# Two heads side by side on the halves of the rows, for the scores of groups two to four

## The chip, the cores and the metric

The kernel runs on one core of one Trainium2 chip. The metric is device time in microseconds (us) of one execution. A core has TensorE (matmuls, with their weight loads), VectorE (DVE), ScalarE (ACT), GpSimd (POOL) and SyncE (SP), and 16 DMA engines. SP and POOL issue nearly all transfers of this kernel.

## The reference

The output joins two results along the last axis. The first is attention with sixteen query heads on one key head and one value head; the second is a filter in the frequency domain.

```python
B, S, D, H = 1, 2048, 448, 16;  Dh = D // H          # Dh = 28
q = (x @ wq).reshape(B, S, H, Dh).transpose(0, 2, 1, 3)
k, v = x @ wk, x @ wv
p = softmax(einsum("bhqd,bkd->bhqk", q, k) * Dh ** -0.5)
a = einsum("bhqk,bkd->bhqd", p, v).transpose(0, 2, 1, 3).reshape(B, S, H * Dh) @ wo
X = rfft2(B_x) * (w_r + 1j * w_i)
b = irfft2(X, s=(S, D))
return concatenate([a, b], axis=-1)
```

All inputs and outputs are float32.

## The kernel before

**Splitting into high and low parts.** Large products run in the one-pass type float32r, which rounds its operands. To keep float32 accuracy an operand is split into a high part (its rounded value) and a low part (the rest). A head has 28 dimensions, padded to 32, so four strips of 32 rows fill the 128 rows of TensorE. The keys lie in `ka`, 128 x 2048: high, high, low, low. A head's queries lie in `qa[c, g][:, h]`, 128 x 512: high, low, high, low. One matmul of 128 rows (L807) sums all four products of the parts.

**Groups, steps, blocks.** The 2048 queries are cut in four chunks `c` of 512 and the sixteen heads in four sets `g` of four. One pair (c, g) is a group; there are sixteen, in the order of `order`. A group has sixteen steps, one for each 128 keys (`kc`), and a step has four scores, one for each head `h`. So there are 256 steps and 1024 scores.

**A score** (`score`, L803): a matmul of 128 keys by 512 queries into one of the seven banks 0 to 6 of PSUM (the one that the plan holds to be free first), then on ScalarE the exp of that bank into a tile `p` (L809). **Values** (`values`, L821): for each step four float32 matmuls of 32 columns, side by side, add the four heads' products into bank 7 (L828). At a group's end VectorE copies bank 7 out (`group_out`, L704), and the next group's values can't start before that copy. Then come the reciprocal of the sums (through DRAM and back, `sd`, `rs`, `rd`, `R`: L709 to L718, issued from POOL) and the norm (L726 to L729).

**The queries of a group** (`build_q`, L166): VectorE makes the high and low parts `qh` and `ql` (L171 to L173). SP issues eight transfers of 64 KB that place them in rows 0 to 63 of the four heads (L182), and one of 512 KB that copies rows 0 to 63 to rows 64 to 127 (L183). The tiles of two groups take turns.

**The frequency part.** A first transform runs ahead of the attention and leaves its result in DRAM (`t1`). During the attention POOL issues eight loads of `X` from it (`spread`, L487), loads of the filters `wf` (L571) and of `wo` (L475). VectorE splits `wo` (L478, L479), and runs the butterflies on `X` and the filter products (L502 to L585). The last transform and the products with `wo` (L738) are done by TensorE between the scores.

**What sets the order.** From L435 on the order of every engine is written out by a planner at build time. It keeps clocks for TensorE, VectorE and ScalarE (`clk`), the times at which banks come free (`free`), and events with due times (`after`). Its main loop (L881) chooses between scores, values and other TensorE work. It holds the scores at most `P_BUFS` = 20 tiles `p` ahead of the values (L887). A block in the steady part is eight scores and two steps of values. The order is fixed at build time: on the chip every engine works through its list and waits where something is not ready.

Of the kernel before, what the change touches and what calls it, by code (L numbers as in the profile page):

```python
# [12 lines left out]
F32 = mybir.dt.float32  # L13
F32R = mybir.dt.float32r
BF16 = mybir.dt.bfloat16
I32 = mybir.dt.int32
AF = mybir.ActivationFunctionType
# [5 lines left out]
S, D, H = 2048, 448, 16  # L23
# [4 lines left out]
CW = 512  # L28
NK = 4
SCALE = DH ** -0.5  # L30
BOUND = float(np.float32(40.0 / SCALE))
P_BUFS = 20
LEAD = 6
WARM = 10, 10


@with_exitstack
def kernel(ctx: ExitStack, tc: tile.TileContext, t: dict):
    nc = tc.nc
    mm = nc.tensor.matmul  # L40
# [13 lines left out]
    ka = cp.tile([128, S], F32R, name="ka")  # L54
# [7 lines left out]
    bank = [bp.tile([128, 512], F32, name=f"b{i}") for i in range(8)]  # L62
# [7 lines left out]
    def spin(*dims):  # L70
        return view(bank[next(turn) % 6], *dims)
# [83 lines left out]
    qa, slots = {}, []  # L155
# [10 lines left out]
    def build_q(c, g, first=False):  # L166
        cs = slice(c * CW, (c + 1) * CW)
        qt = qp.tile([128, CW], F32, name="qt")
        qh = qp.tile([128, CW], F32R, name="qh")
        ql = qp.tile([128, CW], F32R, name="ql")  # L170
        nc.vector.tensor_scalar(qt, qraw[:, g, cs], mask, cvec[:, g, c:c + 1], op0=ALU.mult, op1=ALU.add)  # L171
        nc.vector.tensor_copy(qh, qt)
        nc.vector.tensor_tensor(ql, qt, qh.bitcast(F32), op=ALU.subtract)  # L173
        n = 4 * c + g
        if len(slots) <= n < 2:
            slots.append((qp if n == 0 else ap).tile([128, 4, CW], F32R, name=f"qa{n}", bufs=1))
        q = qa[c, g] = slots[n % 2]
        if first:
            return q, qh, ql
        for i in range(4):  # L180
            for p, src in enumerate((qh, ql)):
                nc.sync.dma_start(q[32 * p:32 * p + 32, i].bitcast(F32), src[32 * i:32 * i + 32].bitcast(F32))  # L182
        nc.sync.dma_start(q[64:128].bitcast(F32), q[0:64].bitcast(F32))  # L183
# [3 lines left out]
    with tc.tile_pool(name="f1", bufs=2) as f1[0], tc.tile_pool(name="w1", bufs=1) as w1:  # L187
# [36 lines left out]
        with tc.tile_pool(name="x1", bufs=2) as x1:  # L224
# [5 lines left out]
            nc.vector.memset(idle, 0.0)  # L230
            for n in WARM:
                nothing = spin(512)
# [94 lines left out]
            for c in range(1, NC):  # L327
                for g in range(NG):
# [22 lines left out]
                    n = 4 * (c - 1) + g  # L351
                    if n in places:
                        q = places.index(n)
# [40 lines left out]
        with tc.If(rv > int(np.float32(BOUND).view(np.int32))), tc.tile_pool(name="g1", bufs=1) as g1:  # L394
# [10 lines left out]
            with tc.For_i(0, 64, 1) as n:  # L405
# [3 lines left out]
                for i in range(4):  # L409
                    r = slice(32 * i, 32 * i + 32)  # L410
# [4 lines left out]
                pt = banks[1][:, :128]  # L415
# [3 lines left out]
            nc.vector.memset(cvec, 0.0)  # L419
            nc.vector.memset(mask, 1.0)  # L420
            parts = build_q(0, 0, True)
            q, qh, ql = parts
            for i in range(4):
# [13 lines left out]
    ap = ctx.enter_context(tc.tile_pool(name="ap", bufs=2))  # L437
    pp = ctx.enter_context(tc.tile_pool(name="pp", bufs=P_BUFS))
# [3 lines left out]
    clk = {"pe": 0.0, "dve": 4.0, "act": 0.0, "mode": "s", "new": False}  # L442
    free = [0.0] * 6 + [2.0]
# [3 lines left out]
    def after(when, dur, f, *a):  # L447
        heapq.heappush(events, (when, next(serial), dur, f, a))

    def vector(until):  # L450
        while clk["dve"] < until:
            if events and events[0][0] <= clk["dve"]:
                _, _, dur, f, a = heapq.heappop(events)
                clk["dve"] += dur
                f(*a)
            elif background and background[0][0] <= clk["dve"]:
                _, dur, f = background.popleft()
                clk["dve"] += dur
                f()
            else:  # L460
                clk["dve"] = min([until] + [x[0] for x in (*events[:1], *list(background)[:1])])
# [5 lines left out]
    wol = ap.tile([128, NG, D], F32R, name="wol", bufs=1)  # L467
    fc["cs3"] = ap.tile([113, 4, 113], F32, name="cs3", bufs=1)
    nc.gpsimd.dma_start(fc["cs3"], t["cs3"])

    wo = {}

# [226 lines left out]
    oh, ol, osb = {}, {}, {}  # L699
# [64 lines left out]
    def switch(mode):  # L764
        if clk["mode"] != mode:
            clk["pe"] += 0.093
            clk["new"] = True
            clk["mode"] = mode

    def spent(dur):  # L770
        if clk["new"] and clk["mode"] == "s":
            dur += 0.105
        clk["new"] = False
        clk["pe"] += dur

    def can_fill():
        return cur[0] is not None or bool(work["z"]) or bool(work["w"])
# [22 lines left out]
    pt, end = {}, [0.0] * 1024  # L800
    EARLY = 6

    def score(i):  # L803
        st, h = divmod(i, 4)
        c, g, kc = steps[st]
        b = min(range(7), key=free.__getitem__)
        mm(bank[b], ka[:, kc * 128:(kc + 1) * 128], qa[c, g][:, h], start=True, stop=True)  # L807
        p = pt[i] = pp.tile([128, CW], F32, name="p")
        nc.scalar.activation(p, bank[b], AF.Exp, scale=SCALE)  # L809
        clk["pe"] = max(clk["pe"], free[b])  # L810
        switch("s")
        a = max(clk["act"], clk["pe"] + 0.54 + (0.1 if clk["new"] else 0.0))
        spent(0.2325)
        clk["act"] = a + 0.477
        end[i] = a + 0.593 + 0.06
        free[b] = a + 0.593 + 0.05
        n = 4 * c + g
        if kc == 0 and h == 0 and n + 1 < len(order):
            after(clk["pe"] + 3.0, 1.7, build_q, *order[n + 1])

    def values(o, n):  # L821
        while taken_out[0] < o // 16:
            vector(clk["dve"] + 0.5)
        switch("v")
        for st in range(o, o + n):
            c, g, kc = steps[st]
            for i in range(4):
                mm(bank[7][32 * i:32 * i + 32], vs[:, kc], pt.pop(4 * st + i), start=(kc == 0), stop=(kc == 15))  # L828
            clk["pe"] = max(clk["pe"], end[4 * st + 3]) + 0.86
            if kc == 15 and st < 255:  # L830
                after(clk["pe"] + 0.4, 0.72, group_out, c, g)
        clk["new"] = False
# [8 lines left out]
    def first_fill():  # L841
        pb = fft1_mm(7)
        clk["pe"] += 1.6
        free[6] = inf
        fft1_out(7, pb)
        clk["dve"] = max(clk["dve"], clk["pe"] + 0.5) + 1.5
        free[6] = clk["dve"] + 0.1

    for g in range(NG):
        after(5.0 + 6 * g, 0.0, wo_load, g)  # L850
        after(11.0 + 6 * g, 1.1, wo_split, g)
# [3 lines left out]
    sc, bt, begun, since, gap = 0, 0, False, 0, 2  # L855
    parts, tail = deque((k, g) for k in range(4) for g in range(NG - 1)), {}

    def partial():
        k, g = parts.popleft()
        if g == 0:  # L860
            b = min(range(7), key=free.__getitem__)
            clk["pe"] = max(clk["pe"], free[b])
            free[b] = inf
            tail[k] = bank[b][:, :D]
        switch("s")
        wo_mm(tail[k], NC - 1, k, (g,))
        spent(0.605)

    def size():
        left = 16 - done_steps % 16  # L870
        rich = sum(map(len, work["w"])) * 0.6 + len(work["z"]) * 0.88 + (len(cur[0][0]) * 0.6 if cur[0] else 0.0) > 1.0
        return left if left < 4 else 2 if left == 4 or not rich else 3
# [3 lines left out]
    def share(n):  # L876
        return max(1.2, 3 * (total - done[0]) / max(250 - done_steps, 3)) if n == 3 else 0.0

    done_steps, quota = 0, 0.0
    n = size()  # L880
    while done_steps < 256:  # L881
        if begun:
            vector(clk["pe"])
        need = 4 * (done_steps + n)
        t_v = end[need - 1] if sc >= need else inf
        soon = min(free) <= clk["pe"] + 0.05
        more = sc < 1024 and sc - 4 * done_steps < P_BUFS  # L887
        if not begun and not soon:
            first_fill()
            begun = True  # L890
        elif t_v <= clk["pe"] + 0.05 and (sc >= min(need + LEAD, 1024) or not soon):
            values(done_steps, n)
            done_steps += n
            n = size()
            since, gap, quota = 0, 2, share(n)
        elif can_fill() and quota > 0 and since >= EARLY and gap >= 2 and (cur[0] or soon):
            t0 = done[0]
            fill()
            quota -= done[0] - t0
            gap = 0  # L900
        elif more and soon:
            score(sc)
            sc += 1
            since += 1
            gap += 1
        elif sc == 1024 and can_fill():
            fill()
        elif sc == 1024 and parts and normed[NC - 1] == NG - 1 and t_v > clk["pe"] + 0.5:
            partial()
        elif t_v <= min(free) or not more:  # L910
            values(done_steps, n)
            done_steps += n
            n = size()
            since, gap, quota = 0, 2, share(n)
        else:
            score(sc)
            sc += 1
            since += 1
            gap += 1
    while can_fill() or events or background:  # L920
        while can_fill():
            fill()
# [2 lines left out]
    c, g = NC - 1, NG - 1  # L925
# [8 lines left out]
    for k in range(4):  # L934
        s = o[:, 128 * k:128 * k + 128]
        r = ap.tile([128, 128], F32, name="r", bufs=1)
# [122 lines left out]
```

## Time and profile before

| what | us |
|---|---|
| median of 3 runs | 649.89 |
| lowest and highest run | 648.18 and 650.11 |
| the profiled execution | 647.86 |
| its span, first to last instruction | 646.0 |
| around the span | 1.86 |
| TensorE busy | 634.9 |
| ScalarE busy | 548.4 |
| VectorE busy | 331.9 |

A row of the profile gives the line of the kernel, the engine, the operation, the tiles written and read, the count, and times. PEld is TensorE's weight load, which overlaps its matmuls. Matmuls are pipelined: their records overlap, and the distance from one start to the next is what a matmul costs in a row of them. The exps overlap in the same way, so that their recorded length is more than what one costs. A row of the timeline shows the start, the length from the first start to the last end, and in brackets the idle time ahead with what ended it. Float32 matmuls appear as two records each.

### The profile page before, as it was taken

The page shows a single profiled execution, that of the slowest core. Times are in us where ns is not written, and L with a number is a line of the kernel's source. Part 1 is how long each engine was busy: PE and PEld are TensorE (multiplying, and loading weights), DVE is VectorE, ACT ScalarE, POOL GpSimd, SP SyncE. Part 2 cuts the span into 40 slices and gives each one's busy share as a digit, 9 for nine tenths or more (in the row PEclk, how much of TensorE's full clock was granted, in tenths as well). Part 3 has the DMA queues.
Part 4 walks back from the last instruction along what each step waited for, and adds up shares of the span by engine and source line. Part 5 has one row for each costly group of instructions (what it writes and reads, how often), then busy time and mean ns, then how long its engine had stood idle before and what let it go on. Part 6 is the DMA issues. An engine that isn't in the chain of part 4 may idle for free.

```text
span 646.0 us, 11674 instructions
## 1 busy us (share of the span) xinstructions
PE 634.9 (98%) x4384; PEld 356.8 (55%) x4384; DVE 331.9 (51%) x685; ACT 548.4 (85%) x1101; POOL 91.0 (14%) x170
## 2 busy tenths in 40 slices
PE   8999899999999989999999999999999999999997
PEld 6877544444444436555445665565555655555654
DVE  6999612599896797887921512130343403120233
ACT  4544899999999978888999888889888798979792
POOL 2021040201011211010131201010201201010100
PEclk9999999999999989999999999999999999999999
DMA  8756499512204322030685231312334231310111
GB/s 276 260 159 176 119 244 192 137 34 51 68 18 105 123 63 64 23 90 15 151 217 149 91 81 46 82 32 65 98 108 113 82 81 31 81 47 1 47 44 57
DMA packets 31162, 63.35 MB, mean 98 GB/s; under 512 B 7093, under 2 KB 18918, under 8 KB 29884
## 3 DMA queue, kind: packets, MB, share of 16 engines
q1 hardware_dynamic: 23168, 39.98, 22.9%
q0 software_dynamic: 7360, 21.69, 12.5%
q8 instruction: 35, 0.57, 0.4%
q10 hardware_dynamic: 576, 0.92, 0.4%
q14 instruction: 23, 0.19, 0.1%
HBM read 30.56 MB, written 15.02 MB: 71 GB/s over the span
## 4 chain that ended last, share of the span: by engine, by line
PE 81%; issue 2%; DVE 2%; DMA 2%; POOL 0%; ACT 0%; ACTq 0%; SPq 0%; DVEq 0%; POOLq 0%
PE b L807 37%; PE b L828 34%; PE b L738 6%; PE b L679 2%; PE b L660 2%; DMA wf<-w 1%; DVE w L579 1%; DMA t<-bs 1%; ACT yb L743 0%; DMA rd<-rs 0%; POOL R L718 0%; DVE X L585 0%; DVE qraw L704 0%; PE b L136 0%; ACTq L748 0%
## 5 line engine op out<-in xcount | busy, mean ns | idle before, releaser
L809 ACT ACTIVATE p<-b 128x512 f32<-128x512 f32 x1024 | 506.9, 743 | 52.2 <-PE b L807 52.2
L807 PE MATMUL b<-qa,ka 128*128 128x512 f32 x1024 | 283.5, 409 | 0.5 <-DVE bs L147 0.5
L807 PEld LDWEIGHTS b<-qa,ka 128*128 128x128 f32 x1024 | 181.6, 188 | 127.3 <-issue 60.5
L828 PE MATMUL b<-p,vs 128*32 128x512 f32 x2048 | 243.6, 601 | 3.2 <-DVE qraw L704 2.9
L828 PEld LDWEIGHTS b<-p,vs 128*32 128x32 f32 x2048 | 55.6, 109 | 127.3 <-issue 122.0
L704 DVE COPY qraw<-b 128x512 f32<-128x512 f32 x15 | 10.3, 690 | 84.6 <-PE b L828 84.6
L709 POOL DMA_DIRECT2D sd<-qraw x15 | 8.9, 590 | 250.5 <-DVE qraw L704 250.5
L746 DVE COPY ya<-b 128x448 f32<-128x448 f32 x12 | 7.5, 624 | 58.9 <-PE b L738 53.4
L544 DVE SCALAR_TENSOR_TENSOR X<-w,X 128x226 f32<-128x226 f32 (+2 forms) x72 | 34.0, 473 | 2.4
L718 POOL DMA_DIRECT2D R<-rd x60 | 29.9, 503 | 35.8 <-DMA rd<-rs 29.2
L666 DVE COPY X<-b 113x512 f32<-113x512 f32 (+1 forms) x16 | 11.1, 692 | 40.8 <-ACT p L809 20.5
L684 DVE COPY X<-b 128x226 f32<-128x226 f32 x16 | 6.2, 390 | 43.2 <-ACT p L809 32.4
L279 PE MATMUL b<-xh,wqh 128*128 128x512 f32 x64 | 25.8, 403 | 0.7 <-ACT wqh L261 0.7
L279 PE MATMUL b<-xh,wql 128*128 128x512 f32 x64 | 25.1, 392 | 0.1
L283 ACT ACTIVATE qraw<-b 128x512 f32<-128x512 f32 x16 | 9.3, 600 | 18.7 <-PE b L279 18.7
L738 PE MATMUL b<-woh,oh 128*128 128x448 f32 x60 | 22.1, 368 | 0.0
L738 PE MATMUL b<-wol,oh 128*128 128x448 f32 x60 | 22.1, 368 | 0.0
L738 PE MATMUL b<-woh,ol 128*128 128x448 f32 x60 | 21.9, 366 | 0.0
L579 DVE TENSOR_TENSOR w<-X,wf 128x904 f32<-128x904 f32 x16 | 17.0, 1093 | 7.1 <-DMA wf<-w 6.9
L715 POOL DMA_DIRECT2D rd<-rs x15 | 8.2, 548 | 82.7 <-DVE rs L714 71.9
L279 PE MATMUL b<-xl,wqh 128*128 128x512 f32 x48 | 18.8, 391 | 0.0
L537 DVE SCALAR_TENSOR_TENSOR w<-X 128x113 f32<-128x113 f32 (+2 forms) x56 | 17.6, 352 | 0.0
(108 smaller groups left out, 516.5 us busy)
## 6 DMA issues: line engine op xcount, KB each, us to landing
qa<-qa SPq DMA_DIRECT2D x15, 512.0 KB, 4.2
X<-t POOLq DMA_DIRECT2D x16, 452.0 KB, 6.2
wf<-w POOLq DMA_DIRECT2D x10, 452.0 KB, 6.5
raw<-xa SPq DMA_DIRECT2D x16, 256.0 KB, 5.2
xb<-xb SPq DMA_DIRECT2D x8, 512.0 KB, 3.9
qa<-qh SPq DMA_DIRECT2D x60, 64.0 KB, 2.0
qa<-ql SPq DMA_DIRECT2D x60, 64.0 KB, 2.2
R<-rd POOLq DMA_DIRECT2D x60, 64.0 KB, 2.2
```

The lines of the kernel that those rows point to most:

```text
L279: mm(pq, w[:, j, gs], x[:, j], start=(j == 0 and n == 0), stop=(j == 3 and n == 1))
L537: STT(out, y, sy, x, op0=ALU.mult, op1=ALU.add if c > 0 else ALU.subtract)
L544: todo(226 * n, lambda d=d, q=q: STT(both(d), t[0].rearrange("p r n f -> p r (n f)"), q, both(a), op0=ALU.mult, op1=ALU.add))
L579: TT(u[r], both(s), wt[k][:, r:r + 1].to_broadcast([128, 2, 452]), op=ALU.mult)
L660: mm(pz[:w, j], c2t[q % 2][:, e, j, :w], fit[q % 2][:, j], start=True, stop=True)
L666: V.tensor_copy(zt[q % 2][e][:w], view(bank[b], 4, 128)[:w].rearrange("p j (r n) -> p r j n", r=2))
L679: mm(py[:, k], z[:w, r, js], fc["cs3"][:w, k], start=True, stop=True)
L718: nc.gpsimd.dma_start(R[32 * i:32 * i + 32], rd[i:i + 1].to_broadcast([32, CW]))
L738: mm(p, x[c][:, g, s], w[:, g], start=(g == 0 and n == 0), stop=(g == NG - 1 and n == 2))
L807: mm(bank[b], ka[:, kc * 128:(kc + 1) * 128], qa[c, g][:, h], start=True, stop=True)
L809: nc.scalar.activation(p, bank[b], AF.Exp, scale=SCALE)
L828: mm(bank[7][32 * i:32 * i + 32], vs[:, kc], pt.pop(4 * st + i), start=(kc == 0), stop=(kc == 15))
```

## The change

In groups two to four (the second, third and fourth set of heads in the first chunk) two heads are scored at once. Head `u` of a pair has rows 64u to 64u+63: its queries' high and low parts. Two new tiles hold key strips: `kh` has the high keys in all four strips, `kl` the low keys. A pair of scores is four matmuls of 64 rows: `kh` for both heads, then `kl` for both heads, each head's two products summed in its own bank. Two exps follow. The tiles `kh` and `kl` use the buffers of `oh` and `ol`, which hold a chunk's normed output later. They are filled by four transfers of 512 KB (64 rows of 8 KB) from `ka`, issued from POOL early in the attention (`strips`). The queries of these groups need no copy of their halves. The planner takes scores in ones or twos and keeps one tile `p` less ahead.

```diff
+HALVED = 4
 def build_q(c, g, first=False):
     ...
+        if n < HALVED:
+            for i in range(4):
+                for p, src in enumerate((qh, ql)):
+                    r = 64 * (i % 2) + 32 * p
+                    nc.sync.dma_start(q[r:r + 32, i // 2].bitcast(F32), src[32 * i:32 * i + 32].bitcast(F32))
+            return
         for i in range(4):
     ...
+    kh = ap.tile([128, S], F32R, name="kh", tag="oh")
+    kl = ap.tile([128, S], F32R, name="kl", tag="ol")
+    def strips():
+        for k, src in ((kh, ka[0:64]), (kl, ka[64:128])):
+            for u in range(2):
+                nc.gpsimd.dma_start(k[64 * u:64 * u + 64].bitcast(F32), src.bitcast(F32))
     ...
 def score(i):
-        b = min(range(7), key=free.__getitem__)
-        mm(bank[b], ka[:, kc * 128:(kc + 1) * 128], qa[c, g][:, h], start=True, stop=True)
-        p = pt[i] = pp.tile([128, CW], F32, name="p")
-        nc.scalar.activation(p, bank[b], AF.Exp, scale=SCALE)
-        clk["pe"] = max(clk["pe"], free[b])
+        n = 4 * c + g
+        pair = 0 < n < HALVED
+        bs = heapq.nsmallest(2 if pair else 1, range(7), key=free.__getitem__)
+        ks = slice(kc * 128, (kc + 1) * 128)
+        if pair:
+            for m, k in enumerate((kh, kl)):
+                for u in range(2):
+                    r = slice(64 * u, 64 * u + 64)
+                    mm(bank[bs[u]], k[r, ks], qa[c, g][r, h // 2], start=(m == 0), stop=(m == 1))
+        else:
+            mm(bank[bs[0]], ka[:, ks], qa[c, g][:, h], start=True, stop=True)
+        for u, b in enumerate(bs):
+            p = pt[i + u] = pp.tile([128, CW], F32, name="p")
+            nc.scalar.activation(p, bank[b], AF.Exp, scale=SCALE)
+        clk["pe"] = max(clk["pe"], *(free[b] for b in bs))
         switch("s")
-        a = max(clk["act"], clk["pe"] + 0.54 + (0.1 if clk["new"] else 0.0))
+        clk["pe"] += 0.2325 * (len(bs) - 1)
+        at = clk["pe"] + 0.54 + (0.1 if clk["new"] else 0.0)
         spent(0.2325)
     ...
+        return len(bs)
     ...
+    after(1.0, 0.0, strips)
     for g in range(NG):
         after(5.0 + 6 * g, 0.0, wo_load, g)
     ...
-        more = sc < 1024 and sc - 4 * done_steps < P_BUFS
+        more = sc < 1024 and sc - 4 * done_steps < P_BUFS - 1
     ...
-            score(sc)
-            sc += 1
-            since += 1
-            gap += 1
+            m = score(sc)
+            sc += m
+            since += m
+            gap += m
```

More of the change, by code (lines that the diff above doesn't have):

```diff
@@ L805, in score @@
         c, g, kc = steps[st]
-        b = min(range(7), key=free.__getitem__)
-        mm(bank[b], ka[:, kc * 128:(kc + 1) * 128], qa[c, g][:, h], start=True, stop=True)
-        p = pt[i] = pp.tile([128, CW], F32, name="p")
-        nc.scalar.activation(p, bank[b], AF.Exp, scale=SCALE)
-        clk["pe"] = max(clk["pe"], free[b])
+        n = 4 * c + g
[13 more added lines that the diff above has]
+        clk["pe"] = max(clk["pe"], *(free[b] for b in bs))
         switch("s")
-        a = max(clk["act"], clk["pe"] + 0.54 + (0.1 if clk["new"] else 0.0))
+        clk["pe"] += 0.2325 * (len(bs) - 1)
+        at = clk["pe"] + 0.54 + (0.1 if clk["new"] else 0.0)
         spent(0.2325)
[L814 to L817, printed above, removed]
+        for u, b in enumerate(bs):
+            a = max(clk["act"], at)
+            clk["act"] = a + 0.477
+            end[i + u] = a + 0.593 + 0.06
+            free[b] = a + 0.593 + 0.05
         if kc == 0 and h == 0 and n + 1 < len(order):
             after(clk["pe"] + 3.0, 1.7, build_q, *order[n + 1])
+        return len(bs)
     def values(o, n):
@@ L915 @@
         else:
[L916 to L919, printed above, removed]
+            m = score(sc)
+            sc += m
+            since += m
+            gap += m
     while can_fill() or events or background:
```

## The prediction

> **What bounds the kernel now.** I read the page first, then the attention stretch by windows and instruction by instruction, then the transfers that run in it.
>
> ```profile
> span 646.0 us, 11674 instructions
> PE 634.9 (98%) x4384; PEld 356.8 (55%) x4384; DVE 331.9 (51%) x685; ACT 548.4 (85%) x1101; POOL 91.0 (14%) x170
> L809 ACT ACTIVATE p<-b 128x512 f32<-128x512 f32 x1024 | 506.9, 743 | 52.2 <-PE b L807 52.2
> 103.30:197.26 93.96, 93.96 (x580) 44.21 (x577) 73.00 (x150) 93.80 (x193) 12.68 (x24) 1.00 0.30 70
> ```
>
> The page makes the kernel look bound by TensorE (98%). The last row is the stretch in which groups two to four are scored (its columns: PE, PEld, DVE, ACT and POOL busy, clock, DMA share, GB/s): there ScalarE is busy for 93.80 of 93.96 us as well. So two engines set the pace. One block of eight scores and two steps of values shows how:
>
> ```profile
> 154.17 0.50 PE L807 MATMUL b<-qa,ka 128*128 128x512 f32 x1
> 154.17 0.73 PE L807 MATMUL b<-qa,ka 128*128 128x512 f32 x2
> 154.17 2.14 PE L807 MATMUL b<-qa,ka 128*128 128x512 f32 x8
> 155.91 0.39 PE L807 MATMUL b<-qa,ka 128*128 128x512 f32 x1
> 156.24 1.92 PE L828 MATMUL b<-p,vs 128*32 128x512 f32 x16
> 158.09 2.14 PE L807 MATMUL b<-qa,ka 128*128 128x512 f32 x8
> 154.76 1.46 ACT L809 ACTIVATE p<-b 128x512 f32<-128x512 f32 x2
> 84.31 1.09 ACT L809 ACTIVATE p<-b 128x512 f32<-128x512 f32 x2
> L809 ACT ACTIVATE p<-b x33: 592/628/741, 79.3 to 95.5; 128x512 f32<-128x512 f32 x33
> 155.78 0.19 PEld L807 LDWEIGHTS b<-qa,ka 128*128 128x128 f32 x1 [0.15 <-ACT p L809]
> ```
>
> Take T = 154.17. The second score starts at T+0.335 (0.73 less its own 0.395), the eighth at T+1.745 (155.91), so six gaps of 0.235 follow the first of 0.335. Values start 0.32 after the eighth score and last 1.85. The block takes 158.09 - 154.17 = 3.92 us. ScalarE: an exp that finds its engine idle takes 0.60 (the minimum is 592 ns; two take 1.09), and the next ends 0.49 later. Eight of them need 8 x 0.49 = 3.92 us, the same figure. Of the seven banks the eighth score reuses the first one of its own block: that exp ends at 154.76 + 1.46 - 0.49 = 155.73, the weight load behind it starts at 155.78, the matmul at 155.91, a hand-over of 0.18.
>
> **Part one: two heads side by side.** In groups two to four 192 full matmuls become 96 pairs of four products. If the two halves of the rows run side by side, a pair needs two passes, as its two scores did before, and TensorE saves nothing. Even if it saved something, ScalarE's 3.92 would stay. Whether float32r products of 64 rows run side by side no row shows. The nearest rows bound it:
>
> ```profile
> 35.26 0.61 PE L136 MATMUL b<-a,fw 64*64 64x226 f32 x8
> L136 PE MATMUL b<-a,fw x16: 351/351/402, 35.3 to 35.9; 64*64 64x226 f32 x16
> ```
>
> Eight records of 0.35 to 0.40 us in 0.61 us: four tiles of 64x64 run at once, on both halves of the rows and into two banks. That end of the bound is a pass of 0.235 for two products. The other end is L807's rate, each product 0.235 by itself: 8 more passes a block, 1.88 us. I take side by side, because L136 has the same halves of the rows.
>
> What does change is when a bank is full. Both banks of a pair are finished by the second pass. The first exp therefore waits for T+0.335+0.395 = T+0.73 (before: T+0.50), starts 0.10 later as now (154.17+0.50 to 154.76), and ends at T+1.43. The built order of TensorE has four pairs and two steps of values in a block, and the second product of the fourth pair goes into the bank that this exp frees. It starts at T+1.43+0.18 = T+1.61, where its turn would be T+0.335+5x0.235 = T+1.51. Its second pass starts at T+1.845, values at T+2.165, the next block at T+4.015: 0.10 more than now. The 193 exps of the window are 24 blocks: 24 x 0.10 = **2.4 us**. Bounds: nothing (a pass some 0.02 shorter, then ScalarE's 3.92 holds) and 24 x 1.88 = 45 us.
>
> The Trainium skill, "TensorE: Matmul & The Clock Gate", Part 3, has four row tiles at 3.07 times one instead of 4; if two tiles lost as much, a pass would be 0.306 and the sum, by that page, some 14 us higher. No run here shows it.
>
> **Part two: four copies in the busiest stretch of the DMA.** The key strips are four copies of 512 KB (64 rows of 8 KB), issued from POOL behind L469 and ahead of all loads of wo, filters and X. Removed is the copy of q's halves (L183) for three groups, the same shape, one at 92.0, one at 113.0, one later.
>
> ```profile
> 84.00:88.00 4.00, 4.00 (x26) 1.88 (x26) 0.78 (x2) 4.00 (x9) 0.00 (x0) 1.00 0.98 306
> 96.00:100.00 4.00, 4.00 (x26) 1.88 (x25) 0.00 (x0) 4.00 (x10) 0.00 (x0) 1.00 1.06 222
> 104.00:108.00 4.00, 4.00 (x26) 1.90 (x25) 0.63 (x1) 3.84 (x9) 0.00 (x0) 1.00 0.98 219
> 108.00:112.00 4.00, 4.00 (x26) 1.94 (x25) 0.06 (x1) 4.00 (x10) 0.59 (x1) 1.00 0.77 145
> 113.00:117.00 4.00, 4.00 (x25) 1.84 (x24) 0.00 (x0) 4.00 (x10) 2.17 (x4) 1.00 0.76 151
> 80.56 0.54 POOL L469 DMA_DIRECT2D cs<-cs  x1 [15.04 <-PE b L807]
> 92.00 0.51 SPq L183 DMA_DIRECT2D qa<-qa  x1
> 113.02 0.50 SPq L183 DMA_DIRECT2D qa<-qa  x1
> ```
>
> From 84 to 108 the 16 engines are full, so what is put in front moves all that follows. Price of one copy: in 113 to 117 the second L183 is nearly all the traffic, 0.76 x 4 = 3.04 us of all engines for 604 KB, so 2.6 us for 512 KB. Four are 10.4 us, less 2.6 for the removed one at 92.0: 7.8 us. VectorE's queue waits on what follows, in this order:
>
> ```profile
> 100.45 0.40 DVE L478 CAST woh<-wo 128x448 fp32r<-128x448 f32 x1 [6.80 <-DMA wo<-wo]
> 101.42 0.54 DVE L171 TENSOR_SCALAR qt<-qraw,mask,cvec 128x512 f32<-128x512 f32 x1
> 102.46 0.69 DVE L173 TENSOR_TENSOR ql<-qt,qh 128x512 fp32r<-128x512 f32 x1
> 107.37 0.69 DVE L704 COPY qraw<-b 128x512 f32<-128x512 f32 x1 [4.21 <-PE b L828]
> 109.25 1.92 PE L828 MATMUL b<-p,vs 128*32 128x512 f32 x16
> 113.38 0.57 POOL L710 DMA_DIRECT2D rs<-sd  x1 [4.44 <-DMA sd<-qraw]
> 113.93 0.51 POOL L487 DMA_DIRECT2D X<-t  x1
> 120.82 1.10 DVE L502 TENSOR_TENSOR X<-X 128x904 f32<-128x904 f32 x1 [12.77 <-DMA X<-t]
> 139.83 0.68 DVE L704 COPY qraw<-b 128x512 f32<-128x512 f32 x1
> 140.43 1.09 DVE L524 TENSOR_TENSOR X<-X,w 128x904 f32<-128x904 f32 x1
> 140.56 1.93 PE L828 MATMUL b<-p,vs 128*32 128x512 f32 x16
> ```
>
> First copy of bank 7 (L704): the last wo lands at about 100.45 + 7.8 = 108.25. Behind it stand its split (0.97 to the next row), q of the third group (1.73, from 101.42 to the end of L173), and the copy (0.69): done at 111.6. Group two's first values wanted bank 7 at 109.25, now 109.45 after two blocks of pairs. TensorE stalls **2.1 us**.
>
> Start of the FFT on VectorE (120.82): the last slice of X is issued (113.93) only after a small transfer queued behind the earlier slices has landed (L710's wait). Everything ahead is 7.8 later; from its issue to 120.82 it took 6.9, of which 2.6 was the L183 copy now gone; idle DMA time in 108 to 117 (0.23 and 0.24 of 4 us) takes up to 1.9 more. 7.8 - 2.6 - a part of 1.9: I take 4.6 us later, between 3 and 7.8.
>
> Second copy of bank 7 (139.83): it starts right behind VectorE's own work, with no wait on TensorE, and ends at 140.51; values start at 140.56. So this copy hangs on the FFT's start with no slack. In the changed build the planner's later TensorE clock also puts one more FFT step (L524's, 1.09) ahead of it. It ends at 140.51+4.6+1.1 = 146.2. TensorE would be there at 140.56+2.4 (shift so far, from 109.25 to 111.65) +8x0.10 = 143.8: a stall of **2.4 us**, TensorE now 5.7 behind. A stall of this kind is in the trace:
>
> ```profile
> 237.54 3.41 PE L828 MATMUL b<-p,vs 128*32 128x512 f32 x16 [2.86 <-DVE qraw L704]
> 237.18:240.59 3.41, 3.04 (x16) 0.59 (x16) 3.41 (x5) 0.38 (x1) 1.14 (x2) 0.50 0.41 99
> ```
>
> After 2.86 us of waiting the granted clock was 0.50 for 3.41 us, and the values behind it took 3.41 instead of 1.92: 1.5 us more. My stall is near that, so I add **1.5 us**. The Trainium skill, same page, Part 1, gives the half clock after at least one idle window of about 3.4 us; by it the added 1.5 would be 0. The trace had it after 2.86.
>
> After that VectorE has room (its third and fourth copies wait for TensorE), and 14 blocks of pairs are left, 1.4 us. The stall at 234 to 237 stays, since its chain starts from the fourth copy:
>
> ```profile
> 201.35 0.69 DVE L704 COPY qraw<-b 128x512 f32<-128x512 f32 x1 [3.33 <-PE b L828]
> 211.86 2.11 DVE L579 TENSOR_TENSOR w<-X,wf 128x904 f32<-128x904 f32 x2 [4.26 <-DMA wf<-w]
> ```
>
> That copy waited 3.33 for TensorE, and the filter loads are issued behind it. q for the pairs costs nothing: the third group's is built at 101.42 and read eight blocks after 103.3, and the last step of its loading is gone. The strips, issued behind L469 at 80.56, need 10.4 us and land at about 95 with the rest of the traffic beside them, before 103.3. The plan's lookahead of 19 instead of 20 changes no block in the built order.
>
> Sum: 5.7 + 1.5 + 1.4 = **8.6 us**. The profiled execution took 647.86 (span 646.0 and 1.86 around it), 2.03 under the median of 649.89. 647.86 + 8.6 = 656.5, which on the median's footing is **658.5 us**.
>
> **Rivals.** (a) The added transfers are hidden: the lanes have room, or loads are spread otherwise than in one line. Against it: shares of 0.98 to 1.06. Only part one is left: 652.3. (b) The halves don't run side by side: 649.89 + 45 = 695; the late copies are then covered by the slower TensorE. For it: no float32r matmul of 64 rows in the trace. Against it: L136. (c) Faster: the stall before 237.54 goes. If TensorE comes later and VectorE doesn't, its fifth copy is done in time; this decides once TensorE's delay exceeds VectorE's by 2.86. With the transfers hidden and 2.4 from the pairs: 649.89 + 2.4 - 2.86 - 1.5 = 647.9, and 645.5 if the pairs cost nothing. Against it: the 3.33 at 201.35 ties VectorE to TensorE there. (d) The effects cancel: no change.
>
> **How the numbers follow.** This kernel's measurement can tell about 0.3%, 2 us, from no change. Forecast 0.68, (a) 0.12, (b) 0.11, (c) 0.05, (d) 0.04. Slower by over 0.3%: forecast, (a) and (b), 0.91; the same 0.04; faster 0.05. The range reaches from (a), 652, to the forecast with the last X 7.8 late instead of 4.6 (3.2 more) and both stalls at the half clock (1.5 more), with some 2 us for estimates: 665. Left out are (b), (c), (d): 0.20.
>
> **What would show it.** Right: blocks of about 4.02 from 103 to 200, with the first exp some 0.83 behind its block's first matmul; DMA share near 1 until about 116; the FFT's first step at 124 to 128; waits of TensorE on L704's line near 110 and 144. Wrong: blocks of 5.8 (halves one after the other), blocks of 3.92 (no bank wait), or the FFT's start still at 121. If the time is under 651, part two is wrong.

## The result and the profile after

| what | before | after |
|---|---|---|
| median of six runs each on one chip, us | 647.88 (646.31 to 650.11) | 653.68 (650.79 to 655.76) |
| ratio of after to before | | 1.008 [1.0055, 1.0106] |
| the profiled execution, us | 647.86 | 650.79 |
| start of the FFT on VectorE, us | 120.82 | 124.50 |
| end of the second copy of bank 7, us | 140.51 | 145.19 |

The changed kernel is slower by 0.8% in the ratio, 5.8 us in the medians. I had forecast 658.5 us, 8.6 more than before: the direction was right, the size was not, since about two thirds of it came. Of the 4.8 us between 658.5 and 653.68, 2.0 is the footing: the forecast stood on a median of 649.89 from three runs of the kernel before, and with six it is 647.88. The profiled execution of the changed kernel is the fastest of its six, 2.9 us under their median; that gap matters below.

In the changed kernel's line numbers the pairs are L830, the single scores L832, the exps L835, the values L857, the copy of bank 7 L720, the strips L485, the loads of X L503, the FFT's first line L518 and the filter products L595. First the page's totals and three of its groups (busy time and mean ns of one, then idle time ahead and what ended it):

```profile
span 649.0 us, 12221 instructions
PE 636.7 (98%) x4576; PEld 360.3 (56%) x4576; DVE 331.9 (51%) x685; ACT 550.3 (85%) x1101; POOL 92.8 (14%) x174
L830 PE MATMUL b<-qa,kh 64*128 64x512 f32 x192 | 42.5, 428 | 0.0
L830 PE MATMUL b<-qa,kl 64*128 64x512 f32 x192 | 40.0, 391 | 0.0
L857 PE MATMUL b<-p,vs 128*32 128x512 f32 x2048 | 242.1, 597 | 5.4 <-DVE qraw L720 5.4
```

The 5.4 us ahead of the values is what TensorE waits for copies of bank 7; it was 2.86, one wait, before. Now one block of pairs, in the timeline of TensorE (start, length of the group, then the row):

```profile
159.09 0.50 PE L830 MATMUL b<-qa,kh 64*128 64x512 f32 x2
159.43 0.39 PE L830 MATMUL b<-qa,kl 64*128 64x512 f32 x2
159.66 0.40 PE L830 MATMUL b<-qa,kh 64*128 64x512 f32 x2
159.90 0.39 PE L830 MATMUL b<-qa,kl 64*128 64x512 f32 x2
160.13 0.39 PE L830 MATMUL b<-qa,kh 64*128 64x512 f32 x2
160.36 0.40 PE L830 MATMUL b<-qa,kl 64*128 64x512 f32 x2
160.60 0.47 PE L830 MATMUL b<-qa,kh 64*128 64x512 f32 x2
160.83 0.47 PE L830 MATMUL b<-qa,kl 64*128 64x512 f32 x2
161.23 1.92 PE L857 MATMUL b<-p,vs 128*32 128x512 f32 x16
163.09 0.50 PE L830 MATMUL b<-qa,kh 64*128 64x512 f32 x2
```

Each row holds two products, one on each half of the rows, and lasts 0.39 to 0.40 us, as long as one full score did (the first row's 0.50 was there before, too). They run side by side, and behind the first a row follows the last by 0.23. Only the fourth pair's two rows last 0.47: there the second product ends 0.08 after the first. I read that as the wait for the bank. The block takes 163.09 - 159.09 = 4.00 us (3.99 in the mean of the blocks without a stall), where it took 3.92.

The transfers, in windows of before's boundaries and one further on (columns: PE, PEld, DVE, ACT and POOL busy, clock, DMA share, GB/s):

```profile
84.00:88.00 4.00, 4.00 (x25) 1.91 (x25) 0.00 (x0) 4.00 (x9) 0.68 (x2) 1.00 1.05 229
96.00:100.00 4.00, 4.00 (x26) 1.89 (x25) 1.02 (x2) 4.00 (x9) 1.53 (x3) 1.00 0.73 210
104.00:108.00 4.00, 4.00 (x33) 2.04 (x34) 1.52 (x4) 3.84 (x9) 0.38 (x1) 1.00 1.04 242
108.00:112.00 4.00, 3.92 (x34) 1.80 (x34) 1.68 (x3) 3.95 (x9) 0.60 (x1) 1.00 1.00 220
113.00:117.00 4.00, 4.00 (x36) 1.97 (x33) 0.00 (x0) 4.00 (x10) 0.00 (x0) 1.00 0.93 200
117.00:121.00 4.00, 4.00 (x36) 1.95 (x33) 0.00 (x0) 4.00 (x10) 2.15 (x4) 1.00 0.55 116
```

But for 96 to 100 the DMA engines are full or nearly so to 117, where before they had slack from 108 on. And what hangs on them, from the timelines of VectorE, POOL and TensorE (the bracket is the idle time ahead with what ended it):

```profile
106.42 0.39 DVE L494 CAST woh<-wo 128x448 fp32r<-128x448 f32 x1 [3.94 <-DMA wo<-wo]
109.03 0.69 DVE L720 COPY qraw<-b 128x512 f32<-128x512 f32 x1
109.77 1.92 PE L857 MATMUL b<-p,vs 128*32 128x512 f32 x16
118.85 0.57 POOL L726 DMA_DIRECT2D rs<-sd  x1 [8.24 <-DMA sd<-qraw]
124.50 1.10 DVE L518 TENSOR_TENSOR X<-X 128x904 f32<-128x904 f32 x1 [14.78 <-DMA X<-t]
144.51 0.68 DVE L720 COPY qraw<-b 128x512 f32<-128x512 f32 x1
145.25 1.92 PE L857 MATMUL b<-p,vs 128*32 128x512 f32 x16 [3.50 <-DVE qraw L720]
207.29 0.69 DVE L720 COPY qraw<-b 128x512 f32<-128x512 f32 x1 [4.27 <-PE b L857]
216.56 2.11 DVE L595 TENSOR_TENSOR w<-X,wf 128x904 f32<-128x904 f32 x2 [3.01 <-DMA wf<-w]
242.41 1.92 PE L857 MATMUL b<-p,vs 128*32 128x512 f32 x16 [1.85 <-DVE qraw L720]
```

Read as a ledger of TensorE's delay against before, in the two profiled executions. At the second copy the values start at 145.25 instead of 140.56, 4.7 late: 3.5 of that is the wait, 1.2 the longer blocks up to there (with 0.1 for the first copy). The blocks after it bring some 1.2 more, so TensorE reaches the fifth copy 5.9 late (242.41 - 1.85 = 240.56; before 237.54 - 2.86 = 234.68). There 1.0 is given back, since the wait is 1.85 instead of 2.86. The values behind it take 1.92 instead of 3.41, since no half clock follows: 1.5 more given back. That leaves 3.4, and 2.9 at the end.

### The profile page after: what moved, and what is told of

Same layout as the page of the kernel before. It is cut to its first block, busy times and chain, and to the rows that moved or that the text cites. A ratio compares the mean times of both kernels' runs of the same rounds, so it can differ in the third digit from the quotient of the medians.

```text
span 649.0 us, 12221 instructions
## 1 busy us (share of the span) xinstructions
PE 636.7 (98%) x4576; PEld 360.3 (56%) x4576; DVE 331.9 (51%) x685; ACT 550.3 (85%) x1101; POOL 92.8 (14%) x174
## 4 chain that ended last, share of the span: by engine, by line
PE 71%; DMA 7%; DVE 6%; issue 2%; ACT 1%; POOL 1%; ACTq 0%; DVEq 0%; POOLq 0%
PE b L857 29%; PE b L832 27%; PE b L754 6%; PE b L830 5%; DMA wo<-wo 2%; PE b L695 2%; PE b L676 2%; DMA wf<-w 1%; DVE w L595 1%; DMA sd<-qraw 1%; DVE X L518 1%; DVE X L519 1%; DMA cs<-cs 1%; ACT p L835 1%; DMA X<-t 1%
## 5 line engine op out<-in xcount | busy, mean ns | idle before, releaser
L835 ACT ACTIVATE p<-b 128x512 f32<-128x512 f32 x1024 | 508.8, 647 | 54.0 <-PE b L832 50.3
L857 PE MATMUL b<-p,vs 128*32 128x512 f32 x2048 | 242.1, 597 | 5.4 <-DVE qraw L720 5.4
L832 PE MATMUL b<-qa,ka 128*128 128x512 f32 x832 | 233.4, 411 | 0.5 <-DVE bs L148 0.5
L832 PEld LDWEIGHTS b<-qa,ka 128*128 128x128 f32 x832 | 148.2, 189 | 96.4 <-issue 39.4
L857 PEld LDWEIGHTS b<-p,vs 128*32 128x32 f32 x2048 | 55.5, 109 | 132.5 <-issue 124.0
L720 DVE COPY qraw<-b 128x512 f32<-128x512 f32 x15 | 10.3, 690 | 80.4 <-PE b L857 80.4
L830 PE MATMUL b<-qa,kh 64*128 64x512 f32 x192 | 42.5, 428 | 0.0
L830 PE MATMUL b<-qa,kl 64*128 64x512 f32 x192 | 40.0, 391 | 0.0
L830 PEld LDWEIGHTS b<-qa,kh 64*128 64x128 f32 x192 | 22.2, 184 | 24.0 <-issue 20.1
L830 PEld LDWEIGHTS b<-qa,kl 64*128 64x128 f32 x192 | 20.1, 185 | 2.1
```

The source lines that it names most:

```text
L720: V.tensor_copy(o, bank[7])
L830: mm(bank[bs[u]], k[r, ks], qa[c, g][r, h // 2], start=(m == 0), stop=(m == 1))
L832: mm(bank[bs[0]], ka[:, ks], qa[c, g][:, h], start=True, stop=True)
```

## The experiments

My theory was that two things cost time: 24 blocks longer by a bank wait, and the strip copies, which push back the FFT, the copy of bank 7 that stands behind it, and so TensorE. The rivals were that the pairs cost nearly all (the copies hidden), and that the copies cost nearly all (the blocks bounded by ScalarE as before). Each ratio below is to the kernel before, run in the same batch (medians 647.65 us for x1 to x4, 647.34 for y1 to y4).

**x1, the copies alone.** The kernel before, with the four strip copies added, read by nobody. The scores stay single and the copy of q's halves stays.

```diff
+    kh = ap.tile([128, S], F32R, name="kh", tag="oh")
+    kl = ap.tile([128, S], F32R, name="kl", tag="ol")
+    def strips(): ...
+    after(1.0, 0.0, strips)
```

> The kernel before with the four strip copies issued as in the change and read by nobody; scores stay single, q keeps its copies, orders of TensorE and VectorE are those of before. Theory (the transfers delay the FFT's start, and the second copy of bank 7 hangs on it): FFT start at 124 to 128 instead of 120.8, TensorE waits 3 to 6 us for the second copy, the blocks stay at 3.92; total +3 to +7 us (more than the change's share, since the q copies are still in the queue), the stall at 235 us stays. Rival (the transfers are hidden, the cost is in the pairs alone): FFT start within 1 us of 120.8, total within 1.5 us of before.

Measured: 657.26 us (655.87 to 659.23), ratio 1.0165 [1.0141, 1.0189]. That is more than the whole change costs, and more than I expected. In its waits and its timeline of TensorE and VectorE:

```profile
PE b L837 <- DVE qraw L713: 5.1, 2, 3.2
PE b L816 <- DMA qa<-qa: 4.4, 1, 4.4
108.22 2.35 PE L816 MATMUL b<-qa,ka 128*128 128x512 f32 x6 [4.42 <-DMA qa<-qa]
109.41 0.40 DVE L487 CAST woh<-wo 128x448 fp32r<-128x448 f32 x1 [8.04 <-DMA wo<-wo]
128.69 1.10 DVE L511 TENSOR_TENSOR X<-X 128x904 f32<-128x904 f32 x1 [14.62 <-DMA X<-t]
108.00:112.00 4.00, 3.78 (x14) 1.80 (x18) 2.49 (x5) 3.05 (x6) 0.00 (x0) 0.61 0.97 219
```

The new wait is group two's first score (L816), which waits 4.42 us for the copy of q's halves: with the strips in the queues SP issues that copy at 98.75 instead of 92.00, and a stretch of low clock (0.61 in the window) follows. The change has no such copy, so it does not have this wait. The last wo is split at 109.41, 9.0 later; four copies, with nothing removed, are 4 x 2.4 = 9.6 us. So the copies do reach VectorE and TensorE. The FFT starts at 128.69, 7.9 later, but that is not the transfers alone: TensorE's wait also makes the first copy of bank 7 late (it ends at 114.08, before at 108.06), and the last X is issued behind it. With the strips in the queue, dropping the copy of q's halves is worth more than the 2.6 us of transfer time that I gave it, since its landing would be waited for too. As a size for the copies within the change, this run is spoilt by the wait that it adds.

**x2, two copies instead of four.** The change, but a half's own rows of `ka` serve as one of its two strips, so that only two copies are needed.

```diff
-        for k, src in ((kh, ka[0:64]), (kl, ka[64:128])):
-            for u in range(2):
-                nc.gpsimd.dma_start(k[64 * u:64 * u + 64].bitcast(F32), src.bitcast(F32))
+        for u in range(2):
+            nc.gpsimd.dma_start(kh[64 - 64 * u:128 - 64 * u].bitcast(F32), ka[64 * u:64 * u + 64].bitcast(F32))
...
-            for m, k in enumerate((kh, kl)):
+            for m in range(2):
...
+                    k = ka if m == u else kh
```

> The change with two strip copies instead of four: head 0 reads its high keys and head 1 its low keys from where they lie already, so only the crosswise halves are copied. Theory: 5 us of DMA work less ahead of X, so the FFT starts at about 119.5 to 121 and the wait for the second copy falls from 3.5 to under 1 us; blocks of pairs stay at 3.99. Total 3 to 5 us under the change, +0.5 to +3 over before. Rival (the one FFT step that was moved ahead of the copy makes the wait): 1.1 us of wait stay, and most of the rest goes. Rival (the cost is in the pairs): no different from the change.

Measured: 648.62 us (646.52 to 650.71), ratio 1.0013 [0.9993, 1.0032]. With half the copies the kernel's time can't be told from that of the kernel before. Its waits and two rows of VectorE:

```profile
PE b L856 <- DVE qraw L718: 1.7, 1, 1.7
121.69 1.10 DVE L516 TENSOR_TENSOR X<-X 128x904 f32<-128x904 f32 x1 [12.09 <-DMA X<-t]
141.71 0.68 DVE L718 COPY qraw<-b 128x512 f32<-128x512 f32 x1
```

The FFT starts at 121.69 instead of 124.50, the second copy is done at 142.39 instead of 145.19, and TensorE waits for one copy only, the fifth. The FFT step that the plan moved ahead of the second copy is still ahead of it, so that step alone does not make the wait. The pairs are still there, with blocks of 3.99. So two of the four copies cost some 4 to 5 us (1.008 against 1.0013 in the ratios, 653.68 against 648.62 in the medians, which come from different batches). The pairs' own price is hidden in the 1.0013: in the trace TensorE is 2.2 us later against before when the last pairs are done than when the first began, and the shorter wait at the fifth copy (1.72, with no half clock) gives 2.7 back.

**x3, the copies stay, but nothing hangs on them.** The change, with a later due time in the planner for the first steps of the FFT, so that fewer of them stand ahead of the second copy of bank 7.

```diff
-                        plain(sa, sb, n, 46.0 if lv == 0 else 0.0)
+                        plain(sa, sb, n, 50.0 if lv == 0 else 0.0)
```

> The change with one number of the plan altered: the FFT's first step is due at 50 instead of 46 on the planner's clock, which puts four FFT steps (4.4 us) behind the second copy of bank 7. Theory: the wait of 3.5 us at the second copy is gone, with nothing changed in the transfers. But the work put off comes back ahead of the fifth copy, where TensorE already waits 1.9 us: that wait grows to some 4 to 5 us. Total within 2 us of the change. Rival (the wait is set by transfers that the copy itself needs): the wait at the second copy stays.

Measured: 647.94 us (644.75 to 649.57), ratio 1.0013 [0.9995, 1.0032]. VectorE's rows:

```profile
125.98 1.10 DVE L518 TENSOR_TENSOR X<-X 128x904 f32<-128x904 f32 x1 [2.10 <-DMA X<-t]
142.30 0.68 DVE L720 COPY qraw<-b 128x512 f32<-128x512 f32 x1
```

All four copies are made and the FFT starts as late as in the change, but twelve of its steps instead of sixteen stand ahead of the second copy. That copy is done at 142.98, and no wait of TensorE for a copy of bank 7 is left. So in the traces the price of the copies was paid in one place: the order of VectorE's queue at 145. I had expected the late wait near 240 to grow, and was wrong: it vanished as well. The ratio therefore mixes two savings. By y1 below the same edit is worth 0.5% to the kernel before, and against y1 this kernel is still 0.6%, some 4 us, slower. The pairs are 2.3 of that; where the rest lies is open, since from the first values to the last its trace takes 552.1 us, as long as y2's with two copies (552.2).

**x4, half the products.** The change without the products with `kl`. It leaves the low part of the keys out of groups two to four.

```diff
-            for m, k in enumerate((kh, kl)):
+            for m, k in ((0, kh),):
...
-                    mm(bank[bs[u]], k[r, ks], qa[c, g][r, h // 2], start=(m == 0), stop=(m == 1))
+                    mm(bank[bs[u]], k[r, ks], qa[c, g][r, h // 2], start=True, stop=True)
```

> The change without the low keys' products: a pair is one pass of two products instead of two passes. The scores of groups two to four leave the low part of the keys out, so this is a test of time alone. Theory (ScalarE holds the block at 8 x 0.49): TensorE has 0.94 us less to do in a block, and the block still takes 3.92, the exps without a gap; 24 x 0.07 = 1.7 us under the change at most. Rival (TensorE sets the block): blocks of about 3.05, some 22 us under the change.

Measured: 653.85 us (652.08 to 654.6), ratio 1.0093 [1.007, 1.0116]. Half of the pairs' products are gone, and no time with them. A block in TensorE's timeline, a window over eleven of them, and the clock behind the second copy:

```profile
157.50 2.13 PE L830 MATMUL b<-qa,kh 64*128 64x512 f32 x8
159.56 1.93 PE L857 MATMUL b<-p,vs 128*32 128x512 f32 x16
161.42 2.13 PE L830 MATMUL b<-qa,kh 64*128 64x512 f32 x8
151.73:198.00 46.27, 46.27 (x288) 17.18 (x287) 40.99 (x105) 46.27 (x97) 6.23 (x12) 1.00 0.14 36
146.73 3.40 PE L857 MATMUL b<-p,vs 128*32 128x512 f32 x16 [4.32 <-DVE qraw L720]
146.30:149.70 3.40, 2.97 (x16) 0.59 (x16) 3.37 (x4) 0.00 (x0) 1.09 (x2) 0.51 0.42 101
```

The block is 161.42 - 157.50 = 3.92 us, and ScalarE is busy for 46.27 of 46.27 us. This is the floor of eight exps at 0.49, so no saving on TensorE could have made these blocks shorter than before. The Trainium skill says of this, in "TensorEngine Tiling (Array Packing)", section "PSUM Bottleneck", that tiling speeds up TensorE but not the emptying of PSUM; the 3.92 agrees. The waits for the copies stayed, 4.32 us at the second, and here a stretch at a clock of 0.51 follows. The blocks are 0.08 shorter, but TensorE's waits for copies add up to 7.8 us instead of 5.4 and two stretches at half clock follow, and the time is that of the change. So this run shows what bounds the blocks, and not what the blocks alone cost.

**y1 and y2, the same later due time for both kernels.** y1 is the kernel before with the edit of x3. y2 is x2 with the edit of x3, so no wait for a copy should be left in either, and their difference is the price of the pairs (with two strip copies).

> The kernel before (single scores, no strips) with the plan's due time of the FFT's first step at 50 instead of 46. It is the partner of the next kernel and a candidate by itself. Theory: the second copy of bank 7 gets slack, and, as the run of the change with the same number showed, the wait of 2.9 us before 237.5 and the half clock behind it go: blocks 3.92 throughout, 3 to 4 us under before, 643.5 to 645. Rival (that wait belongs to the filter loads, not to the order): the wait stays, time as before.

> Pairs with two strip copies and the due time at 50: no transfer delay and no wait for the second copy left, so that the pairs alone differ from the kernel before with the same due time. Theory (the late bank of the fourth pair costs 0.075 a block, 24 blocks, and the two ragged blocks at the ends some 0.4): 2.0 to 2.4 us over that partner, blocks 3.99. Rival (pairs are free, everything was transfers and copies): within 0.5 us of the partner.

Measured: y1 644.43 us (642.92 to 645.64), ratio to before 0.9951 [0.9934, 0.9969]; y2 646.77 us (645.49 to 647.92), ratio 0.9983 [0.9968, 0.9999]. In neither trace does TensorE wait for a copy. Rows of y1:

```profile
230.29 2.13 PE L807 MATMUL b<-qa,ka 128*128 128x512 f32 x8
234.21 1.67 PE L807 MATMUL b<-qa,ka 128*128 128x512 f32 x6
234.37 0.69 DVE L704 COPY qraw<-b 128x512 f32<-128x512 f32 x1 [1.06 <-PE b L828]
```

The fifth copy now waits for TensorE and not TensorE for it; the blocks of single scores are 3.92. The pairs cost 646.77 - 644.43 = 2.3 us, and the two intervals hardly touch. y1 is the best version found: it beats the kernel before by 0.5% and the change by more. It does without the pairs.

**y3 and y4, the late wait by another way.** y3 is the kernel before with the first filter product of each round announced 800 elements longer to the planner; y4 has this and the later due time.

```diff
-            todo(904, lambda r=r: times(r))
+            todo(904 + (800 if r == 0 else 0), lambda r=r: times(r))
```

> The kernel before with only the planned length of the filter products altered (0.86 us more for the first product of each filter), which puts six VectorE steps behind the fifth copy of bank 7, due at 46 as before. Theory (the wait before 237.5 is VectorE's list running behind its plan because of the filter loads): that wait and the half clock behind it go, 3 to 4 us under before. Rival (the copy waits for the loads themselves): no change.

> Both numbers of the plan altered in the kernel before. Theory: one wait can go only once, so it is within 1 us of the better of the two single alterations; work of VectorE is put off further, and the last transform on TensorE may run out of input (a wait after 300 us) if it is too far. Rival (the two add up): 6 us under before.

Measured: y3 645.45 us (643.04 to 646.82), ratio 0.9961 [0.9944, 0.9978]; y4 645.21 us (643.23 to 646.69), ratio 0.9956 [0.9942, 0.9971]. Either edit takes the late wait away and both together bring no more than one. So the late wait with its half clock was worth some 2 to 3 us to the kernel before, where the 2.86 and the 1.5 add up to 4.4. In the trace of y1 it is nearly all there: TensorE gains 4.1 us on before across the fifth copy. But its first values start at 79.58 instead of 77.95, ahead of anything that the edit touches, and so 1.6 of the gain does not show in that execution's time.

## Why the prediction was right or wrong

**Right: side by side, and the bank wait.** Two products on the halves of the rows take one pass. The first exp of a block starts 0.83 behind the block's first matmul, as forecast. The fourth pair's second product comes late, as forecast, but by 0.08 and not 0.10. 24 blocks at 3.99 make 24 x 0.075 = 1.8 us in the trace, and some 0.5 more falls on the shifts from single scores to pairs and back, which the forecast left out. That the 2.3 in the trace, and the 2.3 by y1 and y2, are near the forecast of 2.4 is partly luck. That the bank wait alone makes the longer block was not tried by itself. The rows of 0.47 and x4's 3.92 speak for it.

**Wrong: the shift of 7.8 us.** This is the step that failed first. I priced a strip at 2.6 us by another copy of that size, and took the queue as full throughout. The last wo was split at 106.42, not 108.25: a shift of 6.0. The strips are 256 packets of 8 KB, which took 0.60 us each in the mean, so a copy is 64 x 0.60 / 16 = 2.4 us of all 16 engines. Four of them are 0.8 us less than I took, of the 1.8 that the shift fell short. The rest is open: the window 96 to 100 has a share of 0.73, so the queue was not full throughout, but a new gap makes what follows later and not sooner. The first copy of bank 7 then ended at 109.72, with the values at 109.77. The forecast **stall of 2.1 us is not there**: in the window 108 to 112 TensorE idles for 0.08. This term was a small difference between two large times (111.6 and 109.45), and an error of 1.8 in the one took it away whole.

**Nearly right: the FFT and the second copy.** The FFT came 3.7 later (forecast 4.6, bounds 3 to 7.8), as two errors partly cancelled: the last X was issued 5.5 later instead of 7.8 (119.40 against 113.93), and the FFT began 1.8 sooner behind that issue instead of 3.2. The second copy ended at 145.19 (146.2), with one more FFT step ahead of it. TensorE came to it earlier, at 141.75 instead of 143.8, since the first stall was missing, so the wait is 3.50 instead of 2.4. TensorE's delay there is 4.7 us, where I had 5.7. x2 and x3 show that this is the place where the copies were paid: take either half the copies or four FFT steps from ahead of this copy, and the wait here is gone.

**Wrong: the half clock of 1.5.** The wait was longer than forecast, 3.50 us, and yet no stretch of low clock follows it in the profiled execution of the change. One follows the same wait in x4 (4.32 us, clock 0.51) and two follow waits in x1; waits of 2.68 (x4), 2.86 (before) and 3.22 us (x1) had one. So the length of the wait does not decide. In each of the ten traces all changes of the granted clock (the share of TensorE's full speed) lie a whole number of 3.413 us apart, as if it were decided once in each window of that length. Cut at these points, the traces show how much of each window TensorE was busy (first number behind the length; two windows of the change, then one each of before, x1 and x4):

```profile
139.85:143.26 3.41, 1.89 (x16) 1.23 (x12) 3.38 (x4) 3.41 (x9) 0.00 (x0) 1.00 0.00 0
143.26:146.68 3.42, 1.43 (x16) 0.42 (x16) 3.35 (x6) 1.12 (x3) 0.58 (x1) 1.00 0.24 57
233.77:237.18 3.41, 0.91 (x4) 0.40 (x3) 3.34 (x6) 3.41 (x8) 0.00 (x0) 1.00 0.00 0
105.45:108.86 3.41, 0.64 (x3) 0.60 (x4) 0.00 (x0) 0.13 (x1) 0.00 (x0) 1.00 1.04 223
241.92:245.33 3.41, 0.73 (x9) 0.29 (x12) 3.34 (x7) 2.91 (x6) 0.46 (x1) 1.00 0.12 29
```

In the change the wait lies across two windows, with 1.5 us of idling in one and 2.0 in the next. In the five windows of the attention with a half clock behind them TensorE idled for 2.5 us or more (the last three rows, and one more each of x1 and x4). So where a window ends matters as much as the length of the wait, and I could not have known that ahead: either outcome would have been luck. Idling is not the whole rule: near 71 us, ahead of the attention, eight of the ten traces have a half clock behind a window with only 1.1 to 1.3 us of it. The Trainium skill, "TensorE: Matmul & The Clock Gate", Part 1, says that the gate watches a free-running window of 3413 ns. The spacing of the changes agrees.

**The gap between profile and median.** The six executions of the change fit more such stretches in part: those with a mean granted clock of 0.992 to 0.995 took 653.74 to 655.76 us. But of the three at 0.997 only the profiled one took 650.79; the others took 652.84 and 653.63. Something else differs too. In the ten traces the first values start between 77.7 and 80.2 us, in the change's at 78.00, in x3 and x4 at 80.17 and 79.31, although their edits act only later. I have no trace of the other executions, so what makes up the 2.9 us is not shown.

**Wrong: "The stall at 234 to 237 stays".** It fell from 2.86 to 1.85 and lost its half clock in the profiled execution: 1.0 and 1.5 us given back. The chain did start from the fourth copy (207.29, 5.9 late, as TensorE was), but it got shorter by 1.25: the filter load at 216.56 was waited for 3.01 instead of 4.26. It was issued as far behind the fourth copy as before (5.35 us) but was ready 3.9 instead of 5.2 us after its issue. Why it landed sooner was not isolated. Keeping this stall as it was is a second step that failed: a term of 2.5 us that the sum had at nothing. The rival of a faster kernel was built on this giving back; it came, but for about half of its price and with the second stall beside it.

**The sum.** In the profiled executions: 0.1 for the first stall instead of 2.1, 3.5 instead of 2.4 for the second, 2.3 instead of 2.4 for the pairs, nothing instead of 1.5 for the clock, and 2.5 given back at the late wait, where I had nothing: 3.4, against 8.6. Some 0.5 of that is made up again in the rest of the kernel, mostly behind the last values, and 2.9 is left at the end. The median of the runs has 5.8, and this account covers half of that. The time is 1.4 us from that of the rival "the transfers are hidden" (652.3); on the same footing the rival forecast 2.4 us more than before, against 5.8. Its mechanism was not what happened, since the FFT was late, TensorE waited, and x2 took that wait away by taking copies away.

## What to carry to other kernels

Before two products are put side by side, look at which engine empties their banks: where ScalarE needs as long for its exps as the block lasts, the saving can't show, and filling two banks at once delays the first exp by a pass. A transfer added to a full stretch is paid where the delayed work stands ahead of something the critical engine needs; look for that place in the queue, since moving a few steps there may be worth more than the transfer. A stall that is forecast as a small difference of two large times should get a chance and not a value, and one that stands later in the kernel can give back what an earlier one took.

## What the runs showed of the hardware

Two float32r products of 64 rows by 512 columns, on the two halves of the rows and into two banks, take one pass of 0.23 us together, with no loss beside a full product of 128 rows. A strip copy of 64 rows of 8 KB (512 KB) took 2.4 us of all 16 engines.

The time of one and the same kernel goes with its mean granted clock: over 33 executions of the kernel before, from 0.990 to 0.997, by about 0.49 us for each 0.001 (the correlation is -0.78). One stretch of 3.41 us at half clock is 3.41 x 0.5 / 650 = 0.0026 of the mean, or some 1.3 us by that slope, near the 1.5 that the trace shows behind such a stretch. All changes of the clock in a trace lie a whole number of 3.413 us apart. In the attention a half clock followed five windows of that length in which TensorE had idled for 2.5 to 3.4 us, and none followed the windows in which a wait left up to 2.0 us of idling. One profiled execution of a kernel with TensorE at 98% can stand some 3 us from the median, as that of the change did.
